# Attention scores in two tile shapes within one burst: 256 query columns on 32x128 tiles, the rest on 32x64 tiles

## The chip, the cores and the metric

The kernel runs on one core of one Trainium2 chip. The metric is the device time of one execution in microseconds (us). A core has five engines that run beside each other, each with its own instruction order: PE (TensorE, matrix multiplication; its weight loads are listed apart as PEld), DVE (VectorE), ACT (ScalarE), POOL (GpSimd) and SP (SyncE, which issues most transfers). PE writes its results to banks of PSUM, 512 float32 columns on 128 partitions each; DVE and ACT read them out from there.

A matmul multiplies a stationary block, loaded beforehand as weights, with moving columns. It may use the whole 128x128 array or a tile of it. Here "32x64" means 32 rows (the depth of the sum) and 64 columns (outputs, which become PSUM partitions). Tiles on different rows or columns of the array can work beside each other.

## The reference

One transformer layer on 2048 positions of width 1024, in bfloat16:

```python
H = 32; Dh = D // H; W = 256
q, k, v = qkv[0], qkv[1], qkv[2]
scores = jnp.einsum("bhqd,bhkd->bhqk", q, k) * (Dh ** -0.5)
mask = (idx[:, None] - idx[None, :] >= 0) & (idx[:, None] - idx[None, :] < W)
p = _softmax(jnp.where(mask[None, None], scores, -1e9), axis=-1)
o = jnp.einsum("bhqk,bhkd->bhqd", p, v)
...
h = x + _A_ref(_layernorm(x, axis=-1), A_wqkv, A_wo)
h2 = h + _B_ref(_layernorm(h, axis=-1), B_w1, B_w2)
```

The attention is causal with a sliding window of 256 keys. The 32 heads are 32 wide, so a score sums over 32 numbers only, and four heads can stand on the array's four groups of 32 rows at once. `_B_ref` is a dense layer with 3584 hidden units and silu.

## The kernel before

The sequence is cut into four blocks of 512 positions. PE does, in this order: the projections to v, q and k of a block (`v_group`, `qk_group`), block by block; the output projection (`wo_group`); then per block the two matrix products of the dense layer (`h1_group`, `mm2`). These are dense matmuls: 128x128 weights, 512 moving columns, eight in a row summed into one PSUM bank.

The attention of a block has no stage of its own. Its work is strewn among the dense matmuls of the next block's projections (for the last block, of the output projection). The `Stream` class (L424) keeps this order, written out by hand: `between` (L443) is called ahead of every dense matmul, 192 a block, and as often as is due it first issues a piece of attention output (`attn_out`, L386) that has waited its turn, and then a burst of scores. A block after the first has 20 bursts: four times one `scores_c` and four `scores_xy`. So a burst comes after every nine or ten dense matmuls, and a piece issued with it makes 15 to 24 short matmuls (33 columns each, L392) ahead of the burst.

A burst writes the scores of four heads into four PSUM banks, `sc[0]` (heads 0 and 1) and `sc[1]` (heads 2 and 3). Head `hh` uses the array's rows `hh*32` and up, and its own bank.

- `scores_xy` (L297), the large burst, 48 in the run (three blocks, eight groups of heads, `odd` 0 or 1): 24 matmuls on 32x64 tiles, in three rounds (`step`). A key tile of 128 keys is taken as two halves of 64 keys, one on the first 64 output partitions, one on the others, each with the queries that its keys are seen by. In the first round both halves of the middle key tile `mid` meet 320 queries each, half 0 the queries from `q0`, half 1 those from `q0 + 64`. The second round is 128 queries a half and the third 64, on the tiles `first` and `last`. A round has eight matmuls (four heads, two halves).
- `scores_c` (L330), the small burst, 12 in the run: 16 matmuls on 32x128 tiles, 128 columns each, in four rounds of four.
- `scores_0` (L349) serves the first block alone, on 32x64 tiles.

Behind a large burst ACT reads each pair of banks twice with the exponential (L324, 768 columns, and L325, 256 columns) and writes bfloat16; POOL zeroes the masked triangles (L382, `select`); the result becomes the weights of `attn_out` some bursts later. The banks are single: the next burst's first matmul of heads 0 and 1 waits until ACT has read `sc[0]`, its first of heads 2 and 3 until ACT has read `sc[1]`.

Of the kernel before, what the change touches and what calls it, by code (L numbers as in the profile page):

```python
# [14 lines left out]
P = 128  # L15
# [33 lines left out]
def kernel(  # L49
# [10 lines left out]
    nc = tc.nc  # L60
# [6 lines left out]
    DH = D // H  # L67
# [31 lines left out]
    def view(region, off, *dims):  # L99
        n = 1  # L100
        for d in dims:
            n *= d
        ap = region[:, off:off + n]
        if len(dims) == 2:
            return ap.rearrange("p (a b) -> p a b", b=dims[1])
        if len(dims) == 3:
            return ap.rearrange("p (a b c) -> p a b c", b=dims[1], c=dims[2])
        return ap
# [10 lines left out]
    qT = [view(r_a, (4096, 8192, 12288, 0)[b], G, 512) for b in range(NB)]  # L119
    kT = [view(r_a, 16384 + 4096 * b, G, 512) for b in range(NB)]  # L120
# [176 lines left out]
    def scores_xy(b, g, odd):  # L297
        q0 = odd * P
        mid, first, last = odd, odd - 2, odd + 2

        parts = [
            (mid, 0, q0, q0 + 320, 64), (mid, 1, q0 + 64, q0 + 384, 128),
            (last, 0, q0 + 256, q0 + 384, 384), (first, 1, q0, q0 + 128, 0),
            (first, 0, q0, q0 + 64, 0), (last, 1, q0 + 320, q0 + 384, 448),
        ]
        for step in range(3):
            for hh in range(4):
                for kt, half, qa, qb, col in parts[step * 2:step * 2 + 2]:
                    r0 = hh * DH
                    t = b * 4 + kt  # L310
                    k0 = (t % 4) * P + half * 64
                    nc.tensor.matmul(  # L312
                        sc[hh // 2][half * 64:half * 64 + 64, hh % 2, col:col + qb - qa],
                        lhsT=kT[t // 4][r0:r0 + DH, g, k0:k0 + 64],
                        rhs=qT[b][r0:r0 + DH, g, qa:qb],
                        start=True, stop=True, tile_position=(r0, half * 64),
                    )
        for pair in range(2):
            e = xy_ring[((b * G + g) % 2 * 2 + odd) * 2 + pair]
            tri = e[:, 0:1024].rearrange("p (h c q) -> p h c q", h=2, q=256)  # L320
            bank = sc[pair]
            both = bank[:, :, 0:192]
            both = bass.AP(tensor=both.tensor, offset=both.offset, ap=[*both.ap[:2], [320, 2], both.ap[2]])
            nc.scalar.activation(out=tri[:, :, :, 64:256], in_=both, func=ACT.Exp, scale=scale)  # L324
            nc.scalar.activation(out=e[:, 1024:1280].rearrange("p (h q) -> p h q", q=P), in_=bank[:, :, 192:320], func=ACT.Exp, scale=scale)  # L325
            four = e[:, 0:1024].rearrange("p (c q) -> p c q", q=256)
            select(four[:, :, 0:P], four[:, :, 64:64 + P], False)
            select(four[:, :, P:2 * P], four[:, :, P:2 * P], True)
# [51 lines left out]
    def select(dst, src, upper):  # L380
        sgn = 1 if upper else -1
        nc.gpsimd.affine_select(out=dst, in_=src, pattern=[[0, n] for n in dst.shape[1:-1]] + [[sgn, P]],  # L382
                                compare_op=ALU.is_ge if upper else ALU.is_gt,
                                fill=0.0, base=0, channel_multiplier=-sgn)
# [39 lines left out]
    class Stream:  # L424
# [3 lines left out]
        def __init__(self, b):  # L428
            self.bursts, self.pieces, self.done, self.seen = [], [], 0, 0
            self.behind = 3 if b else 2  # L430
            pending.extend(coming)
            coming.clear()
            for g in range(0, G, 2):
                if b:
                    self.bursts += [lambda g=g: scores_c(b, g)]
                    self.bursts += [lambda g=g, k=k, o=o: scores_xy(b, g + k, o) for k in range(2) for o in range(2)]
                    self.pieces += [lambda g=g, s=s: attn_piece(b, g, *s) for s in SPLIT]
                else:
                    self.bursts += [lambda g=g, k=k, o=o: scores_0(g + k, o) for k in range(2) for o in range(2)]
                    self.pieces += [lambda g=g, k=k: attn_piece(b, g, k, k + 8) for k in range(0, 32, 8)]  # L440
            self.n = len(self.bursts)
# [110 lines left out]
    sc = [sc_pool.tile([P, 2, 512], F32, name=f"sc{i}") for i in range(2)]  # L552
# [212 lines left out]
```

## Time and profile before

The median of three runs is 690.64 us (690.26 to 690.71). The profile is of one more execution:

| what | us |
|---|---|
| span of the profiled execution | 690.4 |
| PE busy | 676.3 |
| PE's weight loads busy | 342.2 |
| DVE busy | 292.3 |
| ACT busy | 244.5 |
| POOL busy | 161.1 |
| first and last start of the large bursts' matmuls | 108.2 and 282.7 |

The granted clock of PE is 1.000 in the whole span. Two things matter for reading it. Matmuls overlap each other, and their ends are modelled; a dense matmul of 512 columns is listed with 379 ns but follows the one before by 216 ns. So durations can't be added up, and times are taken from start to start. And some matmul records are missing from a trace; for instance, a gap of 0.16 us with no cause (`issue`) ahead of a row of eight dense matmuls stands for the ninth that is not listed.

### The profile page before, as it was taken

How to read it: one execution, taken by the hardware profiler on the slowest of the kernel's cores; microseconds unless marked ns; L12 is line 12 of the kernel's file. 1: busy time of each engine (PE TensorE's matmuls, PEld its weight loads, DVE VectorE, ACT ScalarE, POOL GpSimd, SP SyncE). 2: the span in 40 equal slices, each digit the busy share in tenths (PEclk: the TensorE clock that was granted, in tenths of full speed). 3: DMA queues.
4: the chain of work that ended last, by engine and by line, in shares of the span. 5: the costliest groups of instructions: out<-in, count | busy, mean ns of one | idle time of the engine just before them, and what ended most of it. 6: DMA issues, size and time to landing. Idle time of an engine off the chain costs nothing.

```text
span 690.4 us, 14117 instructions
## 1 busy us (share of the span) xinstructions
PE 676.3 (98%) x5890; PEld 342.2 (50%) x6004; DVE 292.3 (42%) x613; ACT 244.5 (35%) x466; POOL 161.1 (23%) x295
## 2 busy tenths in 40 slices
PE   8999999999999999999999999999999999999998
PEld 4445555555555555544444444444444444444445
DVE  5167646744444458443316133343133251333111
ACT  6326666666676667421310033300133100233000
POOL 1007666666666656500000000000000000000000
PEclk9999999999999999999999999999999999999999
DMA  7933142137240888970023310022300124100110
GB/s 249 283 40 93 32 74 75 22 62 188 73 131 17 247 257 248 230 266 32 32 85 108 91 39 0 1 91 70 85 0 1 20 92 94 39 1 1 30 39 24
DMA packets 78640, 61.48 MB, mean 89 GB/s; under 512 B 52464, under 2 KB 62704, under 8 KB 78576
## 3 DMA queue, kind: packets, MB, share of 16 engines
q1 hardware_dynamic: 78432, 60.31, 32.2%
q8 instruction: 47, 0.77, 0.5%
q10 hardware_dynamic: 144, 0.26, 0.1%
q14 instruction: 17, 0.14, 0.1%
HBM read 39.85 MB, written 8.39 MB: 70 GB/s over the span
## 4 chain that ended last, share of the span: by engine, by line
PE 97%; issue 1%; DMA 0%; DVE 0%; DVEq 0%
PE hacc L675 19%; PE acc L259 16%; PE hacc L712 14%; PE acc L712 14%; PE acc L675 9%; PE acc L280 7%; PE acc L249 6%; PE o_ps L392 5%; PE sc L312 3%; PE hacc L280 1%; PE sc L364 1%; PE sc L338 1%; PE o_ps L249 1%; DMA r_o<-in_A_x_dram 0%; PE acc L497 0%
## 5 line engine op out<-in xcount | busy, mean ns | idle before, releaser
L382 POOL TENSOR_SCALAR_AFFINE_SELECT r_e<-r_e 128x512 bf16<-128x512 bf16 (+1 forms) x288 | 158.2, 564 | 124.8 <-ACT r_e L372 61.9
L712 PEld LDWEIGHTS <-r_a 128*128 128x128 bf16 x952 | 90.9, 98 | 103.0
L675 PEld LDWEIGHTS <-r_w 128*128 128x128 bf16 x896 | 87.3, 98 | 105.1 <-issue 0.5
L675 PE MATMUL hacc<-r_e,r_w 128*128 128x512 bf16 x468 | 104.9, 379 | 0.5
L712 PE MATMUL hacc<-r_a 128*128 128x512 bf16 (+1 forms) x496 | 100.2, 361 | 0.4
L324 ACT ACTIVATE r_e<-sc 128x768 bf16<-128x768 f32 x96 | 78.2, 814 | 47.9 <-PE sc L312 47.9
L712 PE MATMUL acc<-r_a 128*128 128x512 bf16 (+1 forms) x439 | 94.5, 372 | 0.5
L684 ACT ACTIVATE r_n<-hacc 128x512 f32<-128x512 f32 x30 | 17.9, 597 | 178.9 <-PE hacc L675 177.8
L259 PEld LDWEIGHTS <-r_w 128*128 128x128 bf16 x512 | 47.1, 98 | 55.0 <-issue 1.0
L261 DVE CAST r_a<-acc 128x512 bf16<-128x512 f32 x56 | 38.7, 692 | 57.0 <-PE acc L259 54.4
L259 PE MATMUL acc<-r_t,r_w 128*128 128x512 bf16 x233 | 56.5, 380 | 2.4 <-issue 1.7
L259 PE MATMUL acc<-r_w 128*128 128x512 bf16 x240 | 56.0, 379 | 1.5 <-issue 0.9
L392 PEld LDWEIGHTS <-r_e 128*128 128x128 bf16 x1440 | 47.4, 96 | 17.9
L392 PE MATMUL o_ps<-r_a,r_e 128*128 128x33 bf16 x1440 | 48.1, 178 | 0.0
L280 PE MATMUL acc<-r_o,r_a 128*128 128x512 bf16 x188 | 46.2, 380 | 1.9 <-issue 1.1
L675 PE MATMUL acc<-r_e,r_w 128*128 128x512 bf16 x191 | 43.3, 379 | 0.2
L727 DVE SCALAR_TENSOR_TENSOR r_t<-acc,r_t 128x512 bf16<-128x512 f32 (+1 forms) x16 | 10.6, 665 | 69.3 <-PE acc L712 69.3
L325 ACT ACTIVATE r_e<-sc 128x256 bf16<-128x256 f32 x96 | 37.5, 390 | 0.0
L280 PEld LDWEIGHTS <-r_a 128*128 128x128 bf16 x256 | 23.4, 98 | 26.9
L685 DVE SCALAR_TENSOR_TENSOR r_a<-r_n,hacc 128x512 bf16<-128x512 f32 x30 | 20.6, 688 | 33.0 <-ACT r_n L684 33.0
L685 DVE SCALAR_TENSOR_TENSOR r_a<-r_a,hacc 128x512 bf16<-128x512 f32 x30 | 20.6, 688 | 31.2 <-ACT r_a L684 31.2
L727 DVE SCALAR_TENSOR_TENSOR r_t<-hacc,r_t 128x512 bf16<-128x512 f32 (+1 forms) x18 | 11.6, 647 | 51.2 <-PE hacc L712 51.2
(103 smaller groups left out, 549.2 us busy)
## 6 DMA issues: line engine op xcount, KB each, us to landing
r_w<-in_B_w_dram SPq DMA_DIRECT2D x8, 896.0 KB, 5.2
r_a<-in_B_w_dram SPq DMA_DIRECT2D x7, 1024.0 KB, 7.5
r_w<-in_A_wqkv_dram SPq DMA_DIRECT2D x4, 1024.0 KB, 9.3
h_dram<-r_t SPq DMA_DIRECT2D x16, 256.0 KB, 2.8
r_t<-h_dram SPq DMA_DIRECT2D x16, 256.0 KB, 2.9
out_dram<-r_t SPq DMA_DIRECT2D x31, 128.0 KB, 1.7
r_o<-in_A_x_dram SPq DMA_DIRECT2D x15, 256.0 KB, 4.4
r_e<-h_dram SPq DMA_DIRECT2D x3, 1024.0 KB, 5.8
```

Of the source, the lines that this page charges most:

```text
L249: nc.tensor.matmul(acc, lhsT=lnT_b[b % 2][:, kt, j * P:(j + 1) * P], rhs=wv[:, kt, c * 512:(c + 1) * 512], start=(kt == 0), stop=(kt == KT ...
L259: nc.tensor.matmul(acc, lhsT=wqk[:, kt, col0:col0 + P], rhs=lnT_b[b % 2][:, kt, :], start=(kt == 0), stop=(kt == KT - 1))
L261: copy(out=(qT, kT)[which][b][:, g, :], in_=acc)
L280: nc.tensor.matmul(acc, lhsT=qT[b][:, g, j * P:(j + 1) * P], rhs=wo[:, g, c * 512:(c + 1) * 512], start=(g == 0), stop=(g == G - 1))
L324: nc.scalar.activation(out=tri[:, :, :, 64:256], in_=both, func=ACT.Exp, scale=scale)
L325: nc.scalar.activation(out=e[:, 1024:1280].rearrange("p (h q) -> p h q", q=P), in_=bank[:, :, 192:320], func=ACT.Exp, scale=scale)
L382: nc.gpsimd.affine_select(out=dst, in_=src, pattern=[[0, n] for n in dst.shape[1:-1]] + [[sgn, P]], compare_op=ALU.is_ge if upper else ALU ...
L392: nc.tensor.matmul(o_ps[pair][:, qt * 2 + hh, 0:VW], lhsT=chunk_of(i, bank, piece, pair, hh), rhs=v[:, b * 4 + kt, g * 4 + pair * 2 + hh, ...
L675: nc.tensor.matmul(acc, lhsT=w1[:, kt, ft * P:(ft + 1) * P], rhs=ln2T[b][:, kt, :], start=(kt == 0), stop=(kt == KT - 1))
L685: nc.vector.scalar_tensor_tensor(out=gT[:, ft, :], in0=th, scalar=1.0, in1=acc, op0=ALU.add, op1=ALU.mult)
L712: nc.tensor.matmul(acc[:, 0:c1 - c0], lhsT=gT[:, ft, j * P:(j + 1) * P], rhs=w2[ft // 4][:, ft % 4, c0:c1], start=(ft == 0), stop=(ft == F ...
L727: nc.vector.scalar_tensor_tensor(out=t_out[j % 2][:, c0:c1], in0=acc[:, 0:c1 - c0], scalar=0.5, in1=t_in[j % 2][:, c0:c1], op0=ALU.mult, o ...
```

## The change

`scores_xy` alone is edited. The middle key tile's 320 queries a half overlap in 256 queries that both halves meet, `q0 + 64` to `q0 + 320`. These become one matmul a head on a 32x128 tile, with all 128 keys as weights: a round of four, ahead of the others. The 64 queries that only half 0 meets (from `q0`) and the 64 that only half 1 meets (from `q0 + 320`) become a round of their own on 32x64 tiles, between the two old ones. A burst is then four matmuls on 32x128 tiles of 256 columns, and 24 on 32x64 tiles: eight of 128 columns, eight of 64, eight of 64. The scores written, their places in PSUM and what reads them are the same.

```diff
         parts = [
-            (mid, 0, q0, q0 + 320, 64), (mid, 1, q0 + 64, q0 + 384, 128),
             (last, 0, q0 + 256, q0 + 384, 384), (first, 1, q0, q0 + 128, 0),
+            (mid, 0, q0, q0 + 64, 64), (mid, 1, q0 + 320, q0 + 384, 384),
             (first, 0, q0, q0 + 64, 0), (last, 1, q0 + 320, q0 + 384, 448),
         ]
+        t = b * 4 + mid
+        for hh in range(4):
+            r0 = hh * DH
+            nc.tensor.matmul(
+                sc[hh // 2][:, hh % 2, 128:384],
+                lhsT=kT[t // 4][r0:r0 + DH, g, (t % 4) * P:(t % 4 + 1) * P],
+                rhs=qT[b][r0:r0 + DH, g, q0 + 64:q0 + 320],
+                start=True, stop=True, tile_position=(r0, 0),
+            )
         for step in range(3):
             for hh in range(4):
                 for kt, half, qa, qb, col in parts[step * 2:step * 2 + 2]:
```

## The prediction

> **What bounds the kernel now.** I read the page first: the span, the engines' shares and the chain that ended last.
>
> ```profile
> span 690.4 us, 14117 instructions
> ...
> PE 676.3 (98%) x5890; PEld 342.2 (50%) x6004; DVE 292.3 (42%) x613; ACT 244.5 (35%) x466; POOL 161.1 (23%) x295
> ...
> PE 97%; issue 1%; DMA 0%; DVE 0%; DVEq 0%
> ```
>
> PE is the bound: 97% of the chain, so whatever time the change adds to or takes from PE's own stream lands in the span nearly one to one. The profiled execution's span, 690.37 us, lies 0.27 below the median of the runs, 690.64, and within their spread (690.26 to 690.71); I put the difference found in the profile onto the median.
>
> Second, the changed line on its own:
>
> ```profile
> L312 PE MATMUL sc<-r_a x1152: 186/214/319, 108.2 to 282.7; 32*64 32x320 bf16 x96, 32*64 32x128 bf16 x48, 32*64 32x64 bf16 x48
> ...
>   ACT r_e L324: 47.9, 48
> ```
>
> 1152 matmuls at 24 a burst are 48 bursts, all between 108 and 283 us. The second line is from the list of who waited: ACT does, for each of the 48, 47.9 us in all, so the exponentials come after the scores and not the scores after them.
>
> Third, the timeline of PE, as narrow as it goes. A query shows what was in flight in a stretch, so asking for stretches a few ns wide separates the rounds. The columns are the start, the length of the merged row, and the instruction. First a large burst whole; then its way in and first round; its second round; its last round and the way out:
>
> ```profile
> 107.65 0.61 PE L392 MATMUL o_ps<-r_a,r_e 128*128 128x33 bf16 x18
> 108.19 0.43 PE L312 MATMUL sc<-r_a 32*64 32x320 bf16 x24
> ```
> ```profile
> 108.08 0.18 PE L392 MATMUL o_ps<-r_a,r_e 128*128 128x33 bf16 x1
> 108.19 0.34 PE L312 MATMUL sc<-r_a 32*64 32x320 bf16 x8
> ```
> ```profile
> 108.35 0.27 PE L312 MATMUL sc<-r_a 32*64 32x128 bf16 x16
> ```
> ```profile
> 108.40 0.21 PE L312 MATMUL sc<-r_a 32*64 32x64 bf16 x8
> 108.55 0.39 PE L249 MATMUL acc<-r_w 128*128 128x512 bf16 x1
> ```
>
> So from the last attention matmul (108.08) it is 0.107 to the first score, 0.160 to the second round, 0.056 to the third and 0.143 to the next dense matmul: 0.466 in all (the rows are rounded to 0.01; the third digit is from the trace's stamps, which are in ns). Within 128x128 work the 18 attention matmuls come 0.025 apart ((108.08 - 107.65) / 17), but the step from them to the first score takes 0.107. Their 33 columns take some 0.014 (33 of the 512 columns for which a dense matmul takes 0.216). So about 0.09 passes in which no new column enters the array: the change of shape costs that. On the way out the last 64 columns take 0.027, and they end some 0.09 before the dense matmul too (the round's eight matmuls start over 0.023).
>
> Fourth, the small bursts, the only ones in the other shape, 32x128:
>
> ```profile
> 105.04 0.18 PE L392 MATMUL o_ps<-r_a,r_e 128*128 128x33 bf16 x1
> 105.15 0.23 PE L338 MATMUL sc<-r_a 32*128 32x128 bf16 x4
> ```
> ```profile
> 105.21 0.34 PE L338 MATMUL sc<-r_a 32*128 32x128 bf16 x12
> ```
> ```profile
> 105.33 0.23 PE L338 MATMUL sc<-r_a 32*128 32x128 bf16 x4
> 105.48 0.39 PE L249 MATMUL acc<-r_w 128*128 128x512 bf16 x1
> ```
>
> Way in 0.110, first round 0.066, the two next ones 0.056 each (105.21 to 105.33 is two), and from the last round's first matmul to the dense one 0.157: 128 columns take 0.053, four starts 0.010, and again some 0.09 of nothing. Both shapes pay it, in and out; it does not depend on which.
>
> **The change, part by part.** A burst computes the same 512 columns per row group as before (320 + 128 + 64 become 256 + 128 + 64 + 64), so no column is saved. Per burst it removes eight 64-wide matmuls of 320 columns, and adds four 128-wide ones of 256 columns and eight 64-wide ones of 64 columns: 28 matmuls and weight loads instead of 24. ACT's, POOL's, DVE's and SP's instructions keep their number and order, and no DMA is moved.
>
> What it adds is a change of shape inside the burst: 32x128, then 32x64. No row of before shows one 32-row shape followed by the other. Its cost is bounded below by zero (the row groups are the same, only the column split differs) and above by the other changes, 0.09 to 0.10. I take the upper end: all four kinds of change that the trace has (128x128 to either 32-row shape, and back from either) cost the same 0.09, however many rows and columns the shapes share.
>
> Step by step, from the last attention matmul to the next dense one:
> - In: 0.110 (the small burst's row), where it was 0.107.
> - The 256-column round up to the first 32x64 matmul: the small burst's way out, 0.157, plus 128 more columns at 0.053, plus the 0.010 by which a first round is longer than a later one (0.066 against 0.056): 0.220.
> - First 32x64 round, 128 columns: a first 320-column round takes 0.160; 192 columns fewer at 0.417 ns (0.216/512, in rounded terms 0.08) leave 0.080. It is the first of its shape, so its weight loads are in front of it as they were in front of the 320 columns.
> - The added 64-column round, up to the last one: 0.028. 64 columns stream in 0.027; the bounds are 0.025 (the attention matmuls' spacing) and 0.056 (a 128-column round, should a 64-wide weight load set the pace).
> - Last round and way out: 0.143, as before.
>
> The sum is 0.581 against 0.466: 0.115 a burst more, of which some 0.09 is the new change of shape and the rest the second first round. Times 48 this is 5.5 us.
>
> The Trainium skill (TensorEngine Tiling (Array Packing), Key Properties) states that a change of tiling mode, not merely of the tile, drains TensorE, and its list of configurations has 32×128 and 32×64 as two. By that rule the sum is the one above; no run here yet shows this pair.
>
> **What waits behind it.** One of the 48 bursts waits for the banks:
>
> ```profile
> 113.67 0.11 PEld L312 LDWEIGHTS <-r_a 32*64 32x64 bf16 x5 [0.42 <-issue]
> 113.95 0.28 PEld L312 LDWEIGHTS <-r_a 32*64 32x64 bf16 x19 [0.17 <-issue]
> ```
>
> It follows dense work alone, and heads 2 and 3 stand 0.28 until ACT has emptied the second pair of banks (its last read, 0.40 long, starts at 113.50). ACT's four reads take about 2.4 us from the burst before, and begin when that burst's scores are written. If the burst ends 0.115 later, ACT ends 0.115 later, and so does the next burst's start: the distance stays. Here the sum is about the same: heads 2 and 3 start after the wait, the change of shape follows them. POOL (564 ns a select, four a burst, against a burst every 3.0 us and more) gets more room; its cover is not used up. The queues of DMA transfers see all dates moved by up to 5.5 us alike.
>
> **The rivals.**
> *No drain between the two 32-row shapes.* For it: in the burst at 113.67 heads 0 and 1 are worked on while 2 and 3 wait, so row groups do not all move together, and both shapes use the same four groups. Against it: the equal 0.09 at every change the trace has. Then the first 32x64 round follows after 0.119 (0.066 + 0.053) and takes 0.056: 0.110 + 0.119 + 0.056 + 0.028 + 0.143 = 0.456, 0.010 less than before, 690.2 us, no change that can be measured. If only the weight loads of the new shape are exposed (0.080 in place of 0.056) it is 0.480, or 691.3. It decides where the change costs under 0.03. The Trainium skill has a rule that points this way (TensorE: Matmul & The Clock Gate, Part 3, The mechanism): weight loads for a row group without conflict, or for the background buffer, are pulled ahead of matmuls in flight. In the trace a burst's loads never start before the change's 0.09 are over.
> *Half of it.* Each row group changes over when it is itself empty: half the 0.09 is saved, 694.0.
> *An added wait for ACT.* Eleven bursts follow nine dense and 15 attention matmuls alone and start 2.54 after the last score of the one before (126.44 to 128.98, for instance), where in the waiting burst the banks were free at 2.45 (111.50 to 113.95): 0.09 to spare. If the later 64-column rounds delay ACT's first read against the burst's end, each may wait up to 0.1: 1.1 us more, 697.3. Against it: the last write to each pair of banks stays in the last round.
> *Faster by over 0.2%.* It takes 0.029 less per burst. With all columns kept, that has to come out of the 0.107 and 0.143 at the ends, which the small bursts show unchanged for the new shape.
>
> **How the numbers follow.** A measurement of this kernel can tell about 0.2%, 1.4 us, from no change. My forecast, the drain, has 0.79; no drain 0.10; half of it 0.04; the wait 0.04; faster 0.03. Slower is drain, half and wait, 0.87; same is no drain, 0.10. The predicted time is 690.64 + 5.5 = 696.2. The drain's own range: a change of 0.08 to 0.10 is 0.5 us either way, the 64-column round at 0.056 adds 1.3: 695.5 to 698.0. To hold 8 in 10 with the half case the range begins at 693.8.
>
> **What would show it.** In the profile after: each large burst as four 32x128 matmuls, then a step of 0.21 to 0.23 to the first 32x64 one, a burst of about 0.35 between first and last start where it was 0.24, the way out unchanged at 0.12 from the last start; ACT's idle time for the scores longer by 48 times 0.1, and dense work after 283 us the same, only later. A step of 0.12 would prove the first rival; starts of single row groups at different distances, the second; more bursts with a gap between heads 1 and 2, the third.

## The result and the profile after

The changed kernel takes 697.82 us (median of four runs, 697.13 to 698.60) against 690.67: a ratio of 1.0100, 95% interval 1.0088 to 1.0112. That is slower by 7.15 us. The forecast was 696.2 us in a range of 693.8 to 698.0: the sign and the range held, and the loss is 1.6 us larger than the sum.

The page of the changed kernel, span, engines and chain:

```profile
span 696.9 us, 14501 instructions
...
PE 678.8 (97%) x6082; PEld 342.7 (49%) x6196; DVE 291.7 (42%) x613; ACT 244.3 (35%) x466; POOL 160.7 (23%) x295
...
PE 94%; DMA 2%; issue 2%; DVE 1%; SPq 0%; DVEq 0%
```

PE's share of the chain fell from 97% to 94%, and transfers (2%) and DVE (1%) stand in it, which had 0% before. Something besides the bursts has come in.

The changed lines (line numbers after the edit are nine higher below it; L309 is the new 32x128 matmul, L321 the 32x64 ones):

```profile
L309 PE MATMUL sc<-r_a x192: 265/278/279, 107.2 to 287.4; 32*128 32x256 bf16 x192
```
```profile
L321 PE MATMUL sc<-r_a x1152: 187/191/239, 107.4 to 287.7; 32*64 32x128 bf16 x96, 32*64 32x64 bf16 x96
...
  ACT r_e L333: 53.2, 47
```

ACT's wait for the scores grew from 47.9 to 53.2 us. The timeline of PE over the first large burst, which ran from 108.19 to 108.55 before:

```profile
106.62 0.61 PE L401 MATMUL o_ps<-r_a,r_e 128*128 128x33 bf16 x18
107.16 0.29 PE L309 MATMUL sc<-r_a 32*128 32x256 bf16 x4
107.37 0.32 PE L321 MATMUL sc<-r_a 32*64 32x128 bf16 x24
107.86 0.38 PE L249 MATMUL acc<-r_w 128*128 128x512 bf16 x1 [0.16 <-issue]
```

The four 32x128 matmuls start together, and the first 32x64 one 0.21 to 0.22 later, though their 256 columns take 0.107. (The dense matmul listed is the second after the burst; the first one's record is missing, as the 0.16 with no cause shows.) From burst to burst the same dense matmul of the two traces moves apart by 0.114 to 0.118 us in 47 of the 48 bursts, and by 0.15 in the one that waits for its banks: 5.60 us in all.

The list of PE's waits has one more thing:

```profile
PE acc L684 <- DMA r_a<-r_a: 1.6, 1, 1.6
```

L684 is the dense layer's first product. It waits 1.6 us for the last of four transposes (`ln_transpose`, L212) that bring the normalized rows to it. The list counts from the modelled end of the matmul before. From start to start the step is 1.98 where two dense matmuls follow each other by 0.216, so PE stood still for 1.76.

The profile of before, where the list of waits has no such row, is not free of it either:

```profile
283.09 1.89 PE L280 MATMUL acc<-r_o,r_a 128*128 128x512 bf16 x8 [0.16 <-issue]
...
285.00 1.42 PEld L675 LDWEIGHTS <-r_w 128*128 128x128 bf16 x8 [0.51 <-issue]
...
285.03 1.89 PE L675 MATMUL acc<-r_a,r_w 128*128 128x512 bf16 x8
```

Eight output projection matmuls from 283.09 on, 0.216 apart, would let the dense layer (L675 there) start at 284.82. It starts at 285.03, 0.21 later, and 0.13 after the landing of its last transpose. In the changed kernel it also starts 0.13 after that landing.

Where the spans of the two first profiles differ, by stretches of the trace (us):

| stretch | before | changed |
|---|---|---|
| start to first small burst | 105.14 | 104.11 |
| from there to the dense layer's second weight load, which starts with its first matmul | 179.89 | 187.43 |
| from there to the end | 405.34 | 405.33 |

The middle one grows by 7.54: the 5.60 of the bursts, 1.55 by which the wait for the transposes is longer (1.76 against 0.21), and 0.40 of three short waits ahead of output projections. The first one scatters by itself: over all profiles of this study it is 103.5 to 105.8 us, while the start's code is the same in all.

One more number for reading the table: in every execution whose span is listed, the time is 1.7 to 1.9 us over the span (698.60 and 696.9 for the profiled one).

### The profile page after: what moved, and what is told of

Its sections match the earlier page's. It is cut to its first block, busy times and chain, and to the rows that moved or that the text cites. A ratio compares the mean times of both kernels' runs of the same rounds, so it can differ in the third digit from the quotient of the medians.

```text
span 696.9 us, 14501 instructions
## 1 busy us (share of the span) xinstructions
PE 678.8 (97%) x6082; PEld 342.7 (49%) x6196; DVE 291.7 (42%) x613; ACT 244.3 (35%) x466; POOL 160.7 (23%) x295
## 4 chain that ended last, share of the span: by engine, by line
PE 94%; DMA 2%; issue 2%; DVE 1%; SPq 0%; DVEq 0%
PE hacc L684 19%; PE acc L259 16%; PE hacc L721 14%; PE acc L721 13%; PE acc L684 8%; PE acc L249 6%; PE o_ps L401 5%; PE acc L280 4%; PE sc L321 2%; PE hacc L280 1%; PE sc L309 1%; DMA h_dram<-r_t 1%; PE sc L373 1%; DMA r_a<-r_a 1%; DMA r_w<-in_A_wqkv_dram 1%
## 5 line engine op out<-in xcount | busy, mean ns | idle before, releaser
L684 PEld LDWEIGHTS <-r_w 128*128 128x128 bf16 x896 | 87.1, 98 | 106.8 <-issue 2.1
L684 PE MATMUL hacc<-r_e,r_w 128*128 128x512 bf16 x468 | 104.9, 379 | 0.5
L333 ACT ACTIVATE r_e<-sc 128x768 bf16<-128x768 f32 x96 | 78.2, 814 | 54.0 <-PE sc L321 53.2
L684 PE MATMUL acc<-r_e,r_w 128*128 128x512 bf16 x191 | 43.4, 379 | 0.2
```

What stands on the lines that cost most here:

```text
L684: nc.tensor.matmul(acc, lhsT=w1[:, kt, ft * P:(ft + 1) * P], rhs=ln2T[b][:, kt, :], start=(kt == 0), stop=(kt == KT - 1))
```

## The experiments

Times are compared with runs of the kernel before on the same chip in the same job: 690.95 us (16 runs) for the two kernels again, the split on one shape and the rounds on 32x128; 690.77 (13 runs) for two changes, the other way round and the earlier transposes; 690.86 (7 runs) for every second burst and the later load; and 691.03 (15 runs) for the last. The theory is that PE is empty for some 0.09 us whenever its tile shape changes, 32x128 to 32x64 included. The rivals: the added round and weight loads are the cost; only some kinds of change cost; and, for the part beyond 5.6 us, the start or the wait for the transposes.

**The two kernels again, unchanged.** 

> The kernel before, unchanged, for a second profile of it: are its start and its way into the dense layer the same from run to run? In its first profile the dense layer's first matmul starts 0.05 us after the last output projection, with no wait for a transfer; in the changed kernel's it waits 1.6 us for the transposes. If that wait comes from transfers that land when they will, this profile shows some of it too, anything from 0 to 1.5 us; if it belongs to the change, none. The large bursts: 0.24 us from first to last start, 48 times.

> The changed kernel, unchanged, for a second profile and more times. Theory (a drain between 32x128 and 32x64, 0.115 us in each of 48 bursts): 5.5 us over before again, whatever the rest does. The rest of the measured 7.15 is the wait ahead of the dense layer: if it is chance, this profile has another value for it (0 to 1.5 us) and the times scatter over about as much; if it belongs to the change, 1.5 us again.

Before again took 690.87 us, with a span of 689.1; its first small burst started at 103.58, 1.57 earlier than in the first profile, and its dense layer did not wait. Changed again took 697.82 us (697.42 to 698.47), the profiled execution 698.09. It has no wait for the transposes either, but a start of 105.73. From the first small burst to the dense layer it takes 185.27, 5.1 to 5.4 more than the two profiles of before (179.89 and 180.15, which have 0.2 and 0.5 of short waits themselves). So the bursts' 5.60 repeat, and start and wait change from profile to profile. The times of the changed kernel do not reach down to 696.5, though, in eight runs, so the two profiles alone did not settle where the rest is.

**The same split on one shape.** The 256 columns, too, on 32x64 tiles (edits of the bursts are shown against the changed kernel):

```diff
         parts = [
+            (mid, 0, q0 + 64, q0 + 320, 128), (mid, 1, q0 + 64, q0 + 320, 128),
             (last, 0, q0 + 256, q0 + 384, 384), (first, 1, q0, q0 + 128, 0),
...
-        t = b * 4 + mid
-        for hh in range(4):
-            r0 = hh * DH
-            nc.tensor.matmul(
...
-        for step in range(3):
+        for step in range(len(parts) // 2):
```

> The same split of the queries (256 that both halves meet, 64 and 64 apart), but the 256 columns too on 32x64 tiles, so a burst has 32 matmuls in four rounds and no change of shape inside. Theory (the drain is the cost): 0.107 + 0.133 + 0.056 + 0.028 + 0.143 = 0.467 against 0.466, so 690.7, the same as before. Rival (the added round and weight loads are the cost, not the shape): 0.1 us a burst as in the changed kernel, 695 to 696.

```profile
111.35 0.61 PE L393 MATMUL o_ps<-r_a,r_e 128*128 128x33 bf16 x18
111.90 0.43 PE L313 MATMUL sc<-r_a 32*64 32x256 bf16 x32
112.26 0.61 PE L249 MATMUL acc<-r_w 128*128 128x512 bf16 x2
```

This is the timeline of PE over one of its bursts: 32 matmuls in four rounds take 0.36 from the first one to the dense matmul, as 24 did before. Start to start, a burst is 0.005 longer (0.24 us for 48 of them). So neither the added round nor the added weight loads are the price. The time, though, is 693.35 us (691.82 to 694.75; ratio 1.0035, 1.0022 to 1.0048), which missed both expectations. This profile, of an execution of 694.75, has a late start (105.77) and this wait:

```profile
PE acc L676 <- DMA r_a<-r_a: 1.0, 1, 1.0
```

From start to start that wait is 1.1, and some 0.8 of short waits ahead of output projections stand in the same profile. So a kernel whose bursts are as long as before has the wait for the transposes too: it does not need the changed shape.

**All rounds on 32x128 tiles.** The three rounds on 32x64 tiles give way to two on 32x128 tiles, 128 keys by 128 queries each, of `last` and `first`. The kernel leaves out the right pairing of keys and queries, so part of its scores are wrong; it serves for the time alone. Of the two loops added, the lines that differ from the loop over `mid`:

```diff
+        t = b * 4 + last
...
+                sc[hh // 2][:, hh % 2, 384:384 + 384 - 256],
...
+                rhs=qT[b][r0:r0 + DH, g, q0 + 256:q0 + 384],
...
+        t = b * 4 + first
...
+                sc[hh // 2][:, hh % 2, 0:0 + 128 - 0],
...
+                rhs=qT[b][r0:r0 + DH, g, q0 + 0:q0 + 128],
...
-        for step in range(3):
...
```

> All rounds of the large burst on 32x128 tiles: 256, 128 and 128 columns, 12 matmuls, the same 512 columns, no change of shape inside. The halves that meet different queries get the same ones, so some scores are of the wrong keys or queries: the text leaves the right pairing out to have one shape. Theory (drain): 0.110 + 0.119 + 0.056 + 0.157 = 0.442 against 0.466, 48 times -0.024: 689.5. Rival (128-wide tiles beside each other are slow here in themselves, whatever follows): still above before, 692 or more.

```profile
109.62 0.62 PE L402 MATMUL o_ps<-r_a,r_e 128*128 128x33 bf16 x18
110.17 0.29 PE L304 MATMUL sc<-r_a 32*128 32x256 bf16 x4
110.28 0.22 PE L313 MATMUL sc<-r_a 32*128 32x128 bf16 x4
110.34 0.23 PE L322 MATMUL sc<-r_a 32*128 32x128 bf16 x4
110.50 0.82 PE L249 MATMUL acc<-r_w 128*128 128x512 bf16 x3
```

The same 256 columns as in the changed kernel are followed after 0.12 by the next round, when that keeps the shape. The burst is about 0.02 shorter than before, as expected. The time did not follow: 691.41 us (689.80 to 692.91), no difference from before (ratio 1.0004, 0.9992 to 1.0016). The profile has the wait for the transposes again, 0.9 us by the list, and 0.6 of short waits ahead of output projections, so what the bursts gave (about 1.2 us) was given back there. In four of its ten runs, 689.80 to 690.32, the gain shows.

**Two changes of shape instead of one.** The rounds in the order 32x64, 32x128, 32x64: the loop over `step` stands once ahead of the 32x128 matmuls, for the 128 columns, and once behind them, for the rest.

```diff
         parts = [
             (last, 0, q0 + 256, q0 + 384, 384), (first, 1, q0, q0 + 128, 0),
+        ]
+        for step in range(len(parts) // 2):
...
         t = b * 4 + mid
...
+        parts = [
             (mid, 0, q0, q0 + 64, 64), (mid, 1, q0 + 320, q0 + 384, 384),
             (first, 0, q0, q0 + 64, 0), (last, 1, q0 + 320, q0 + 384, 448),
         ]
-        for step in range(3):
+        for step in range(len(parts) // 2):
...
```

> The changed burst with its rounds in another order: 128 columns on 32x64 tiles first, then the 256 on 32x128, then 64 and 64 on 32x64: two changes of shape inside instead of one. Theory (0.09 a change): into the first round 0.107, to the 256 columns 0.196, to the next 32x64 round 0.220, to the last round 0.054, out 0.143, in all 0.720 against 0.466: 48 times 0.254 is 12.2 us over before in the bursts, so twice what the changed kernel's bursts take, 703 to 705 with the 0 to 2 us that the start and the way into the dense layer add. Rival (one exposed set of weight loads, not a drain): 5.5 to 7 us, as in the changed kernel, 697 to 698.

```profile
106.21 0.61 PE L415 MATMUL o_ps<-r_a,r_e 128*128 128x33 bf16 x18
106.74 0.26 PE L310 MATMUL sc<-r_a 32*64 32x128 bf16 x8
106.94 0.29 PE L319 MATMUL sc<-r_a 32*128 32x256 bf16 x4
107.15 0.27 PE L335 MATMUL sc<-r_a 32*64 32x64 bf16 x16
107.35 0.82 PE L249 MATMUL acc<-r_w 128*128 128x512 bf16 x3
```

From the first score to the dense matmul it is 0.61, where it was 0.36. Each of the 48 bursts is 0.252 longer than before, against 0.254 forecast: 12.1 us. The time is 702.73 us (702.52 to 703.08; ratio 1.0175), 12.0 over before. No wait for the transposes is listed in this profile. Twice the changes, about twice the price: the rival of 5.5 to 7 us is out.

**The other way round.** 32x64 rounds first, the 256 columns last; the loop over the 32x128 matmuls is moved behind the other:

```diff
-        t = b * 4 + mid
-        for hh in range(4):
...
-        for step in range(3):
+        for step in range(len(parts) // 2):
...
+        t = b * 4 + mid
+        for hh in range(4):
...
```

> The changed burst with the 32x64 rounds first and the 256 columns on 32x128 last: one change of shape inside, the other way round. Theory (a drain, either way): 0.107 + 0.080 + 0.028 + 0.143 + 0.220 = 0.578 against 0.466, 5.4 us over before in the bursts, 0.1 less than the changed kernel, 696 to 698. Rival (only 64-wide weight loads behind 128-wide ones wait): 0.09 a burst less, about 691 to 692.

```profile
109.98 0.61 PE L401 MATMUL o_ps<-r_a,r_e 128*128 128x33 bf16 x18
110.53 0.32 PE L312 MATMUL sc<-r_a 32*64 32x128 bf16 x24
110.78 0.29 PE L321 MATMUL sc<-r_a 32*128 32x256 bf16 x4
111.00 0.60 PE L249 MATMUL acc<-r_w 128*128 128x512 bf16 x2
```

The bursts are 0.116 longer each, the same as in the changed kernel and 0.004 more than forecast; 697.13 us (695.95 to 697.82), with a wait of 1.1 us for the transposes in the profile. The direction of the change does not matter.

**The change in every second burst.**

```diff
+        if odd:
+            parts = [
+                (mid, 0, q0, q0 + 320, 64), (mid, 1, q0 + 64, q0 + 384, 128),
+                (last, 0, q0 + 256, q0 + 384, 384), (first, 1, q0, q0 + 128, 0),
+                (first, 0, q0, q0 + 64, 0), (last, 1, q0 + 320, q0 + 384, 448),
+            ]
+        else:
+            t = b * 4 + mid
+            for hh in range(4):
...
```

> The change in every second large burst alone (odd = 0), 24 of the 48. Theory (a fixed price per changed burst, 0.116 as measured): 2.8 us over before in the bursts, 693.5 to 695 with 0 to 1.5 us of waits at the start and ahead of the dense layer. Rival (the price comes of all bursts running late one behind another, ACT or POOL falling behind): less than half of it, under 2 us in the bursts.

In the trace 24 bursts are 0.116 longer and 24 are as before: 2.8 us. The time is 694.60 us (693.73 to 695.88), 3.7 over before; the profile, of the fastest of its runs, has a wait of 0.5 us for the transposes. The price is one per changed burst; no backlog of ACT or POOL takes part.

**The transposes earlier.** In both kernels, the steps of the normalization ahead of the dense layer are taken three at a time from the 18th output projection on, so the last transposes are issued one projection earlier:

```diff
-        for _ in range(1 if n < 14 else 2):
+        for _ in range(1 if n < 14 else 2 if n < 17 else 3):
```

> The kernel before, with the last transposes ahead of the dense layer issued one output projection earlier (about 2.5 us; three steps of the normalization at a time from the 18th projection on). The dense layer's first matmul did not wait for them in two profiles, so: same, 690.3 to 691.2, and no wait in the profile.

> The changed kernel with the same earlier transposes. If the 1.4 us that the change costs beyond its bursts are a wait for those transposes, they go: 5.5 us over before early, 696.0 to 696.6, scattered less. If they come from the start (the clock that is granted later), nothing moves: 697.8.

Before early: 690.78 us, the same as before (ratio 1.0001, 0.9992 to 1.0011). Changed early: 696.77 us (695.92 to 697.08), 6.0 over before early, and no wait for the transposes in the profile. All four runs lie below all eight of the changed kernel, which come from other jobs; the kernel before differs by under 0.4 us between the jobs (690.67 to 691.03). So that wait was about 1 of the 1.5 us that the bursts leave open. The time came out 0.2 above the range expected. The profile shows where that can come from: 0.73 of short waits ahead of three output projections, which before early does not have.

**The load ahead of the transposes.** The changed kernel, with the load of the first part of `w2` (1 MB) issued behind the last transposes instead of ahead of them:

```diff
-        if n == 17:
+        if n == 21:
             nc.sync.dma_start(out=w2[0], in_=w2_v[:, 0:4, :])
```

> The changed kernel, with the load of the first 1 MB of the second dense weights issued four output projections later, behind the last transposes instead of ahead of them. The transfers' share is full in the 15 us ahead of the dense layer; if this load is what the transposes queue behind, the wait ahead of the dense layer goes and the time falls to 696.0 to 696.8, as with the earlier transposes. If other transfers (residual rows, stores, the first dense weights) hold them up, 697.2 to 698 as before.

First the order in SP's queue in the changed kernel, where L665 is that load and the four L212 `r_a<-r_a` are the transposes:

```profile
274.69 0.39 SPq L665 DMA_DIRECT2D r_a<-in_B_w_dram  x1
276.42 1.23 SPq L212 DMA_TRANSPOSE r_a<-r_a  x1
...
279.06 2.13 SPq L212 DMA_TRANSPOSE r_a<-r_a  x1
...
282.60 2.19 SPq L212 DMA_TRANSPOSE r_a<-r_a  x1
...
285.99 1.23 SPq L212 DMA_TRANSPOSE r_a<-r_a  x1
```

With the load moved back:

```profile
276.10 1.23 SPq L212 DMA_TRANSPOSE r_a<-r_a  x1
...
278.53 1.23 SPq L212 DMA_TRANSPOSE r_a<-r_a  x1
...
281.17 1.82 SPq L212 DMA_TRANSPOSE r_a<-r_a  x1
...
284.20 1.23 SPq L212 DMA_TRANSPOSE r_a<-r_a  x1
285.53 0.53 SPq L665 DMA_DIRECT2D r_a<-in_B_w_dram  x1
```

The hold-ups of 2.1 and 2.2 are gone, one of 1.8 has come in, the last transpose is issued 8.1 after the first instead of 9.6, and the dense layer does not wait. The time is 696.53 us (695.98 to 696.72), 5.67 over before (ratio 1.0077, 1.0061 to 1.0094), and its stretch from the first small burst to the dense layer is 185.27, 5.60 more than in the profile of before early (179.67). That is the bursts' 5.60 and nothing else. It shows that the wait goes when the load is moved, and not how the load acts: it had landed by 280.8 in the changed kernel, ahead of the second hold-up (282.60) and of the last transpose (285.99).

**The same in the kernel before.** The same edit, without the change of shape:

> The kernel before, with the same later load of the second dense weights. Its dense layer did not wait in the profiles, so the transposes seem to land in time most of the time there: same as before, 690.4 to 690.9. If some of its slower executions (up to 692.3) are ones with that wait, the highest times go and the median falls by up to 0.3.

690.79 us (690.52 to 691.45; ratio 0.9996, 0.9987 to 1.0005): the same. The highest times did not come up (691.45 against 692.83), which eleven runs leave open to chance, and the median is not lower beyond its interval. No version here beats the kernel before by more than the measurement can tell.

## Why the prediction was right, and where it fell short

- *PE is the bound and what is added lands in the span.* Right: 5.60 us in the bursts, and 5.67 us in the time once the wait for the transposes is out of the way.
- *The change of shape inside the burst costs the upper end, 0.09.* Right, and shown by five kernels that differ in the bursts alone: no inner change, the same length as before (0.005) or 0.02 less; one, 0.116; two, 0.252; one in reverse, 0.116. These lengths hold some 0.03 of added rounds besides the changes. The Trainium skill's rule (TensorEngine Tiling (Array Packing), Key Properties), that changing the tiling mode drains TensorE, holds for this pair; the trace prices it at about 0.09 us. The burst that waits for its banks shows that the change waits for all four heads: there the 32x128 matmuls of heads 0 and 1 start at 112.87 and those of heads 2 and 3 at 113.17 and 113.18, and the first 32x64 one at 113.39. That is 0.21 after the last 32x128 one, as in the first burst (107.165 to 107.374), though heads 0 and 1 had their 0.107 of columns behind them at 112.98. What exactly empties in the 0.09 us themselves was not tried.
- *The sum, step by step.* Way in 0.110 (0.110 forecast); the 256 columns to the first 32x64 matmul 0.218 (0.220); first round 0.080 (0.080); added round 0.029 (0.028); last round and way out 0.146 (0.143). In all 0.583 against 0.466 before, by these steps 0.117; the dense matmuls' distance gives 0.116 in all but one burst, where 0.115 was forecast.
- *The rivals.* No drain and half a drain are out by the same numbers, and half a drain also by the burst above, in which no head changes over on its own; so is the Trainium skill's rule that weight loads are pulled ahead (TensorE: Matmul & The Clock Gate, Part 3) as an argument against the drain: here it did not shorten a change of shape. In the first burst the first 32x64 weight load starts at 107.37 with its matmul, 0.10 after the last 32x128 columns are through. The added wait for ACT did not come: the burst that waited for the banks before is there with 0.30 between heads 1 and 2 instead of 0.28, and no others show one. One reading beside it is off: bursts follow each other by 2.4 us once and by 2.8 eleven times, not by 3.0 and more; four selects of 564 ns still fit.
- *"The queues of DMA transfers see all dates moved by up to 5.5 us alike."* This is the step that failed. The transposes ahead of the dense layer came later against PE's own work, and PE waited 1.76 us for them in one profile and not at all in another. In the times this is 1.0 to 1.3 us (697.82 against 696.77 and 696.53). The forecast gave this wait no term, because the list of waits of before had no row for it; it did not ask how much room that start had. There was none: in that very profile the dense layer started 0.21 late, on the landing of its last transpose, and in the second one of before the landing left 0.37 of room.
- *The range.* That 697.82 lies in it is luck in part. Its upper end has 1.3 us for an added 64-column round of 0.056; the round took 0.029, and a wait that the forecast did not have filled that place. The drain with its round at 0.028 gave at most 696.7, which the kernel with the later load meets (696.53).
- *The profiled execution against the median.* The prediction put the difference onto the median, which is sound, but it compared a span (690.37) with times. A later execution of the kernel before with a span of 690.4 took 692.22 us. So the first profile was of an execution about 1.5 us slower than the median, with a late start and the 0.21 of wait. The size of the bursts did not hang on it.

What stays open: why the transposes come late so often in kernels with an edit in the bursts, even where these are no longer. From start to start the wait was 0.65 to 1.76 us in five profiles of such kernels and nothing in two with the load in its old place, against 0.21 and nothing in the two of the unchanged kernel before. In four of the five the last transpose landed 5.2 to 5.5 us after its issue began, in the fifth (32x64 throughout) after 4.3, with the last one issued 10.0 after the first; in all other profiles it landed after 3.1 to 4.3. What lengthens the landing is not shown.

## What to carry to other kernels

In this kernel each change of tile shape in PE's stream has cost about 0.09 us in which no column entered, whichever two of its three shapes met, so a burst of small matmuls here does best to keep one shape from end to end, even where another shape needs fewer matmuls for a part of it. Before counting a gain or a loss on PE as the whole effect, look for the places where PE starts on data that has only just arrived: "no wait" in one profile's list says nothing of the room there, and the list leaves out the first 0.16 us of a wait behind a dense matmul, which is listed with 379 ns and followed after 216. Compare the step from start to start with the usual one. Where a bulk load is issued ahead of a short transfer that PE will need next, it is worth trying to move it: here that took 1.3 us off the changed kernel, and nothing measurable off the kernel before.

## What the runs showed that was not expected

- Row groups did not keep the order of the instructions among each other in one burst, all of it on one shape. In the burst before the change that waits for its second pair of banks, the last 64-column matmuls of heads 0 and 1 start 0.38 after the burst's first, ahead of the 128-column matmuls of heads 2 and 3 at 0.42, which come earlier in PE's stream.
- Eight matmuls on different tiles start 0.0033 apart, and a first round on 32x64 tiles is 0.027 longer than its columns, on 32x128 tiles 0.013. That is eight and four starts at 0.0033; why a first round alone is longer by them is not shown.
- The start up to the first small burst takes 103.5 to 105.8 us with the same code. This alone is as large as many changes that one would want to measure. It goes along with PE's clock: the granted clock of 1.000 in the profile of before comes from a record that begins 8.7 us into the span. There, dense matmuls of 512 columns follow each other by 0.40 to 0.43 up to 8.5 us, and by 0.21 to 0.22 from 9.4 on. In 12 profiles the trace has such a record; it begins at 4.2 to 7.1 us in nine of them, with the first small burst at 103.5 to 104.3, and at 8.7 to 10.3 in the three with the latest (105.15, 105.73 and 105.78).
